# A planner's model of the chip: measured durations, tiling changes, DMA rate and clock, with due times fitted anew

## The chip, the cores and the metric

The kernel runs on one core of one Trainium2 chip. The core has TensorE (PE, matmuls; PEld is its weight load), VectorE (DVE), ScalarE (ACT), GpSimd (POOL) and SyncE (SP), which here issues every DMA. Each engine works through its own queue in order; a semaphore holds an instruction until its inputs are there, and everything behind it on that engine waits too. The metric is the device time of one execution in microseconds (us), lower is better; a profiled execution has a span, from its first to its last instruction.

## What is computed

A recurrent attention over 768 steps for 4 batches of 8 heads with head size 40, and then a two-branch MLP over the 3072 tokens:

```python
for t in range(S):                                   # S = 768, state (B, H, 40, 40)
    y[:, :, t] = einsum('bhd,bhde->bhe', rt, state)
    Sa = einsum('bhde,bhe->bhd', state, at)
    state = state * wt[:, :, None, :] - einsum('bhd,bhe->bhde', Sa, bt) + einsum('bhd,bhe->bhde', vt, kt)
x = y.transpose(0, 2, 1, 3).reshape(3072, 320)
out = ((x @ w1) * (x @ w2) @ w3) @ w_out             # 320 -> 1024 -> 1024 -> 320
```

The MLP weights arrive as 64-bit floats.

## The kernel before

The 768 steps are cut into 12 **chunks** of 64 steps; a chunk has 4 **groups** (one for each batch, 8 heads each). The work of the whole kernel is cut into a few thousand *ops*, each a handful of instructions on one engine:

- **Weight conversion** (`convert`, L277 to L301): 33 pieces of 128x512. SP loads `raw` (L277); DVE takes the exponent `e` (L280), the high mantissa (L290), adds the low word (L294) and forms the sign and exponent factor `sg` (L298); ACT does L284 and L287; POOL multiplies (L301). Four pieces are of w1 and w2, five of w_out, sixteen of w3, eight more of w1 and w2. PE multiplies w3 and w_out into one matrix (L354), and L341 makes the low halves of w1 and w2. No MLP can begin before all of this is done (the mark `W12`).
- **scale** (L384 to L411), for each group: running products of the decays `fm` on DVE, log and exponential on ACT (L393, L396), the scaled inputs `lh` and `fm` on DVE or POOL.
- **causal** (L436): products inside the chunk on PE; ACT copies them to `JP` and `lh`; POOL masks (L454).
- **solve** (L468 to L546), once a chunk: L468 transposes `JP` into `ab`, some fifty DVE instructions invert triangular blocks, L543 and L546 write `TDX`. **join** (L569, L576): PE and ACT make `TT` from it.
- **pairs** (L613) and **tokens** (L636): products and transposes that need no state.
- **rec**, for each group, the only part that carries the state from chunk to chunk: L652, L659, L666, L677 and the transpose L700 on PE, with ACT copies and the DVE steps L670, L694, L711 between.
- **mlp**, once a chunk: 16 sets of 8 matmuls 128x128 by 256 columns (L763), ACT and DVE steps on their results, 8 sets of 6 matmuls by 320 columns (L789), and the stores. Its input `xs` is made by ACT (L746) and DVE (L749) from what `gather` (L721) has brought together by DMA.

L176 is the copy helper of ACT. The PE array is used as a whole (L354, L636, L652, L700, L763, L789), as 128-row halves of 64 columns (L659, L677), as 64x64 quarters (L436, L613, L666) or as 32x32 blocks (L569, L576). Below, a **tiling change** is a place where two ops that follow each other on PE use the array in different ones of these four ways.

What sets the order is a **planner**, the class `Order`. All ops are first recorded with engine, cost, due time, what they read and write, and their buffers; `place` then plays the chip on the host: each engine has a clock, an op can start when its engine, its inputs and its buffers are free, and of the ops of an engine that could start first the one with the earliest due time is taken. An op marked `two` uses the SBUF port that DVE and POOL share and isn't planned beside one of the other engine. The sequence that comes out is fixed for each engine in the program. The core of it:

```python
first = min(t for t, _ in starts)
o = min((o for t, o in starts if t <= first + 1e-9), key=lambda o: (o["due"], o["n"]))
cost = o["cost"]
if e == "pe":
    cost += 0.1 * (o["kind"] != last)
clock[e] = t + cost
done = clock[e] + LAT[e]
u["ready"] = max(u["ready"], clock[e] if u["eng"] == e != "sp" else done)
```

Due times are a start per chunk (`T0 + T * c`) plus an offset per stage (the table `P`); a DMA is planned at 0.4 to 0.6 us with 3 us more until its data are there.

Of the kernel before, what the change touches and what calls it, by code (L numbers as in the profile page):

```python
# [18 lines left out]
C = 64  # L19
# [11 lines left out]
LAT = dict(pe=0.33, act=0.09, dve=0.09, pool=0.1, sp=3.0, nil=0.0)  # L31
# [9 lines left out]
ON = dict(cv="p", ws="d", lh="dpdddppdpdpp", xs="pppdpppdpppd", gl="pppdpppddddd")  # L41

# [14 lines left out]
class Order:  # L57
# [14 lines left out]
    def op(self, eng, cost, due, fn, r=(), w=(), two=False, kind=None, hold=()):  # L72
# [13 lines left out]
        for s in slots:  # L86
            s.left += 1
        self.ops.append(dict(n=n, eng=eng, cost=cost, due=due, fn=fn, deps=deps - {None, n}, slots=slots, two=two,
                             kind=kind))

    def place(self):
        ops = self.ops
        for o in ops:
            o["users"], o["wait"] = [], len(o["deps"])
        for o in ops:
            for d in o["deps"]:
                ops[d]["users"].append(o)
        free = {p: [(0.0, i) for i in range(n)] for p, n in SLOTS.items()}
        ready = {e: [] for e in LAT}
        clock, last, lock = dict.fromkeys(LAT, 0.0), None, {"dve": 0.0, "pool": 0.0}  # L100
        for o in ops:
            o["ready"] = 0.0
            if not o["wait"]:
                ready[o["eng"]].append(o)

        def begin(o):

            t, new = max(o["ready"], clock[o["eng"]]), {}
# [8 lines left out]
            if o["two"]:  # L117
                t = max(t, lock["pool" if o["eng"] == "dve" else "dve"])
            return t

        placed = []
        while len(placed) < len(ops):
            best = None
            for e in LAT:
                starts = [(t, o) for o in ready[e] if (t := begin(o)) is not None]
                if starts:
                    first = min(t for t, _ in starts)
                    o = min((o for t, o in starts if t <= first + 1e-9), key=lambda o: (o["due"], o["n"]))
                    if best is None or first < best[0]:
                        best = first, o  # L130
# [6 lines left out]
            if e == "pe":  # L137
                cost += 0.1 * (o["kind"] != last)
                last = o["kind"]
# [6 lines left out]
            if o["two"]:  # L146
                lock[e] = clock[e]
# [816 lines left out]
```

## Time and profile before

| | |
|---|---|
| time, median of 3 runs | 757.23 us (756.07 to 763.5) |
| span of the profiled execution | 757.2 us |
| PE busy / DVE / ACT / POOL | 84% / 79% / 62% / 32% |
| moved by DMA | 70.44 MB, 93 GB/s over the span |
| mean granted TensorE clock | 0.966 |

The profiled execution's own time and its span are the same number within 0.1 us, and both are the median of the runs. Busy shares are averages over a first part, in which weights are converted beside the first chunks, and a second, in which MLP and attention share PE. Times of an instruction in a timeline are from its start on its engine to its end; matmuls are pipelined, so from one set of matmuls to the next the start times count, not the durations.

### The profile page before, as it was taken

The page shows a single profiled execution, that of the slowest core. Times are in us where ns is not written, and L with a number is a line of the kernel's source. Part 1 is how long each engine was busy: PE and PEld are TensorE (multiplying, and loading weights), DVE is VectorE, ACT ScalarE, POOL GpSimd, SP SyncE. Part 2 cuts the span into 40 slices and gives each one's busy share as a digit, 9 for nine tenths or more (in the row PEclk, how much of TensorE's full clock was granted, in tenths as well). Part 3 has the DMA queues.
Part 4 walks back from the last instruction along what each step waited for, and adds up shares of the span by engine and source line. Part 5 has one row for each costly group of instructions (what it writes and reads, how often), then busy time and mean ns, then how long its engine had stood idle before and what let it go on. Part 6 is the DMA issues. An engine that isn't in the chain of part 4 may idle for free.

```text
span 757.2 us, 22430 instructions
## 1 busy us (share of the span) xinstructions
PE 635.4 (84%) x9106; PEld 565.1 (75%) x9106; DVE 598.8 (79%) x1177; ACT 471.3 (62%) x1127; POOL 245.1 (32%) x326
## 2 busy tenths in 40 slices
PE   0411198874889999999999999999999999999996
PEld 0301176653778898898898889888989889999996
DVE  5779979999989995995887979969788789595421
ACT  2653486655876577687676785867757767646321
POOL 2444454333324142353341323715324213100000
PEclk9999999876779999999999999999999999999999
DMA  8922257433340241433333323333343243120010
GB/s 212 262 68 94 84 140 226 138 102 112 102 122 16 55 124 51 116 84 81 96 91 101 83 73 104 85 83 84 82 107 91 66 103 100 40 57 23 11 35 21
DMA packets 57947, 70.44 MB, mean 93 GB/s; under 512 B 30960, under 2 KB 38640, under 8 KB 57840
## 3 DMA queue, kind: packets, MB, share of 16 engines
q1 hardware_dynamic: 57840, 68.97, 33.7%
q8 instruction: 73, 1.20, 0.7%
q14 instruction: 34, 0.28, 0.1%
HBM read 60.29 MB, written 3.93 MB: 85 GB/s over the span
## 4 chain that ended last, share of the span: by engine, by line
PE 42%; DVE 23%; ACT 4%; DMA 4%; issue 3%; SPq 1%; POOL 0%; DVEq 0%; POOLq 0%; ACTq 0%
PE bank L763 16%; PE bank L789 7%; DVE tmp L494 3%; DMA fm<-in_fmx_dram 3%; PE bank L659 3%; PE bank L652 3%; PE bank L677 3%; PE bank L666 3%; DVE xu L670 2%; PE bank L613 2%; PE bank L436 2%; PE bank L636 2%; PE bank L700 1%; ACT TT L176 1%; DVE ab L468 1%
## 5 line engine op out<-in xcount | busy, mean ns | idle before, releaser
L763 PE MATMUL bank<-xs,W 128*128 128x256 f32 x1536 | 212.1, 288 | 3.4 <-DVE ga L777 1.4
L763 PEld LDWEIGHTS bank<-xs,W 128*128 128x128 f32 x1536 | 189.2, 189 | 10.3 <-DVE ga L777 1.7
L176 ACT ACTIVATE xu<-bank 64x256 f32<-64x256 f32 (+2 forms) x184 | 80.0, 440 | 25.6 <-PE bank L613 13.0
L454 POOL TENSOR_SCALAR_AFFINE_SELECT lh<-lh 64x256 f32<-64x256 f32 x96 | 44.4, 462 | 149.5 <-ACT lh L176 125.0
L176 ACT ACTIVATE JP<-bank 32x256 f32<-32x256 f32 (+1 forms) x216 | 75.5, 350 | 14.3 <-PE bank L436 10.3
L670 DVE TENSOR_TENSOR xu<-bank,mask_h 64x416 f32<-64x416 f32 x96 | 56.2, 586 | 33.9 <-PE bank L666 31.8
L621 POOL TENSOR_SCALAR_AFFINE_SELECT xu<-xu 64x256 f32<-64x256 f32 x96 | 43.9, 457 | 111.1 <-ACT xu L176 91.0
L411 POOL TENSOR_TENSOR fm<-fm,gi 104x512 f32<-104x512 f32 x36 | 51.2, 1423 | 45.2 <-DVE gi L407 36.6
L659 PE MATMUL bank<-xu,lh 104*64 104x104 f32 (+2 forms) x768 | 50.6, 272 | 16.4 <-POOL xu L621 14.2
L789 PE MATMUL bank<-W3h,gh 128*128 128x320 f32 x192 | 64.2, 334 | 0.0
L436 PE MATMUL bank<-lh,fm 40*64 40x64 f32 x1536 | 38.5, 240 | 26.6 <-POOL fm L411 23.4
L789 PE MATMUL bank<-W3l,gh 128*128 128x320 f32 x192 | 59.3, 309 | 0.0
L789 PE MATMUL bank<-W3h,gl 128*128 128x320 f32 x192 | 59.1, 308 | 0.0
L613 PE MATMUL bank<-rv 40*64 40x64 f32 x768 | 34.5, 232 | 27.9 <-DMA rv<-in_rv_dram 18.7
L659 PEld LDWEIGHTS bank<-xu,lh 104*64 104x64 f32 (+2 forms) x768 | 40.4, 146 | 23.2 <-POOL xu L621 15.0
L436 PEld LDWEIGHTS bank<-lh,fm 40*64 40x64 f32 x1536 | 31.4, 148 | 33.1 <-POOL fm L411 24.0
L777 DVE TENSOR_TENSOR ga<-bank,ga 128x512 f32<-128x512 f32 x48 | 32.8, 684 | 27.4 <-PE bank L763 25.9
L613 PEld LDWEIGHTS bank<-rv 40*64 40x64 f32 x768 | 27.7, 141 | 35.7 <-DMA rv<-in_rv_dram 18.0
L284 ACT ACTIVATE e<-e,ebias 128x512 uint16<-128x512 uint16 x33 | 23.3, 717 | 47.2 <-DVE e L280 47.1
L666 PE MATMUL bank<-hs,TT 64*64 64x104 f32 x768 | 47.4, 268 | 4.7 <-ACT TT L176 2.1
L176 ACT ACTIVATE gh<-ga 128x512 fp32r<-128x512 f32 x48 | 30.1, 627 | 33.5 <-DVE ga L777 33.4
L176 ACT ACTIVATE ga<-bank 128x512 f32<-128x512 f32 x48 | 28.6, 595 | 31.6 <-PE bank L763 31.3
(96 smaller groups left out, 1448.6 us busy)
## 6 DMA issues: line engine op xcount, KB each, us to landing
fm<-in_fmx_dram SPq DMA_DIRECT2D x48, 313.6 KB
rv<-in_rv_dram SPq DMA_DIRECT2D x48, 273.0 KB
lh<-in_fma_dram SPq DMA_DIRECT2D x48, 208.0 KB
raw<-in_w3t_dram SPq DMA_DIRECT2D x16, 512.0 KB
raw<-in_w_dram SPq DMA_DIRECT2D x12, 512.0 KB
xu<-in_vt_dram SPq DMA_DIRECT2D x96, 40.0 KB
out_dram<-o SPq DMA_DIRECT2D x48, 80.0 KB
xr<-y SPq DMA_DIRECT2D x72, 40.0 KB
```

Source lines behind the costliest of these rows:

```text
L176: act.activation(out_, in_, AF.Copy, scale=scale)
L411: e.tensor_tensor(out=X, in0=X, in1=gi.t.unsqueeze(2).to_broadcast([104, NP, 2, C]), op=ALU.mult)
L436: pe.matmul(out=bank(ab)[64 * x:64 * x + 64, p], lhsT=X[r, p, x], rhs=lh.t[r, ab, p], start=True, stop=True)
L454: pool.affine_select(out=lh.t[q, ab], in_=lh.t[q, ab], pattern=[[0, NP], [1, C]], compare_op=ALU.is_gt, fill=0.0, base=0, channel_multipli ...
L613: pe.matmul(out=bank()[64 - 64 * ab:128 - 64 * ab, p, 0:C], lhsT=rvt.t[r, p, C + D:], rhs=rvt.t[r, p, 0:C], start=True, stop=True)
L621: op("pool", 0.5, due + 2, lambda q=q, ab=ab: pool.affine_select(out=xu.t[q, ab, :, 0:C], in_=xu.t[q, ab, :, 0:C], pattern=[[0, NP], [1, C ...
L659: pe.matmul(out=view(hp)[64 * ab:64 * ab + 64, p], lhsT=lh.t[k, ab, p], rhs=xu.t[k, ab, p], start=True, stop=True)
L666: pe.matmul(out=view(hh)[r, p], lhsT=tt.t[r, n0 + p], rhs=hs.t[r, p], start=True, stop=True)
L670: dve.tensor_tensor(out=xu.t[r, ab], in0=view(hh)[r], in1=mask_h[r].unsqueeze(1).to_broadcast([64, NP, N]), op=ALU.mult)
L763: pe.matmul(out=pt.t[:, TOK * x:TOK * x + TOK], lhsT=WT[k][:, cs], rhs=xs.t[:, z], start=(n == 0), stop=(n == 7))
L777: op("dve", 0.65, t, lambda a=a, pt=pt: dve.tensor_tensor(out=a.t, in0=wide(pt), in1=a.t, op=ALU.mult), r=[pt], w=[a])
L789: pe.matmul(out=pt.t[:, 0:DM], lhsT=l.t[:, j, ts], rhs=W3[r][:, j], start=(j == 0 and n == 0), stop=(j == NJ - 1 and n == 2))
```

## The change

No instruction of the computation is changed, nor how many there are of one, nor on which engine it is, nor a buffer count. Changed are the numbers and rules by which `place` orders them: a table `OPS` gives each of some seventy kinds of op its duration (and for PE the way it uses the array and the time to its last result); a table `OFF` adds an offset to the due time of each kind; `LAT` has a lag for each pair of engines; a DMA occupies its queue for a time that follows its bytes; a PE op in another tiling has to wait until the one before is finished (`turn`) and pays an entry (`ENTRY`); and the planned PE has two clock levels, set by how busy its plan has been. Of ops that could start within `LOOK` of the first (0.092 us on PE, 0.046 us on POOL), the one due first is taken. `T0`, `T` and `P` have new values. All calls of `op` name a kind in place of engine and cost.

```diff
-LAT = dict(pe=0.33, act=0.09, dve=0.09, pool=0.1, sp=3.0, nil=0.0)
-T0, T = 29.92, 49.86
-P = dict(w0=13.0, ws=3.12, ld=74.57, sc=51.76, ca=50.45, so=7.57, sp=36.91, jo=6.89, pa=12.28, tk=4.63, rg=14.44,
-         ga=35.51, ml=82.44, mt=47.69)
+T0, T = 37.797, 51.192
+P = dict(w0=11.454, ws=3.321, ld=32.264, sc=51.261, ca=85.143, so=7.546, sp=49.375, jo=113.483, pa=26.202, tk=12.035,
+         rg=12.467, ga=112.137, ml=87.719, mt=49.172)
+OFF = {"ca.jd": -119.786, "ca.jo": -52.948, "ca.lh": 12.039, "ca.mask": -5.365, "ca.mm": -117.544, "cv.e": 6.804,
+       "cv.exp": 61.542, "cv.f": 6.953, "cv.in": 36.478, "cv.lo": 13.503, "cv.m": -184.82, "cv.out/p": -153.603,
...
+LOOK = dict(pe=0.092, act=0.0, dve=0.0, pool=0.046, sp=0.0, nil=0.0)
...
+OPS = {
+    "cv.in": ("sp", 2.23), "cv.e": ("dve", 0.415, 1), "cv.exp": ("act", 0.72), "cv.sign": ("act", 0.66),
...
+    "ld.fm": ("sp", 1.4), "ld.lh": ("sp", 0.93),
...
+    "r.mm2": ("pe", 0.714, 0, "c64", 0.884), "r.hs": ("act", 0.517), "r.mm3": ("pe", 0.71, 0, "64", 0.88),
...
+ENTRY = {"128": 0.09, "c64": 0.04, "64": 0.04, "32": 0.0}
...
-            t, new = max(o["ready"], clock[o["eng"]]), {}
+            t, new = max(o["ready"], turn if e == "pe" and o["mode"] != last else clock[e]), {}
...
-                    o = min((o for t, o in starts if t <= first + 1e-9), key=lambda o: (o["due"], o["n"]))
+                    t, o = min(((t, o) for t, o in starts if t <= first + LOOK[e]), key=lambda x: (x[1]["due"], x[1]["n"]))
...
-            cost = o["cost"]
-            if e == "pe":
-                cost += 0.1 * (o["kind"] != last)
-                last = o["kind"]
+            if e == "pe":
...
+                f = 1 if hot else 2
+                begun = t + f * ENTRY[o["mode"]] * (o["mode"] != last)
+                done, last = begun + f * o["span"], o["mode"]
+                clock[e], turn = begun + f * o["cost"], done - 0.07
...
-        op("dve", 0.4, due, f1, w=[G])
-        op("dve", 0.72, due, f2, w=[G], two=True)
+        op("sc.min", due, f1, w=[G])
+        op("sc.scan", due, f2, w=[G])
```

The changed file is 55 lines longer from the table on: L384 of before is L439 of the changed one, and so on with every line below.

Where the order differs, in three places. **ACT, before its copies into `JP` for the third and fourth group of the first chunk** (L176 is the copy, L284 and L287 belong to the weight conversion, L393 and L396 to scale). Before:

```order
L284 ACTIVATE e_153<-e_153,ebias 128x512
L176 ACTIVATE xu_119<-bank_140 64x4x64
L393 ACTIVATE gi_110<-fm_100 104x256
L396 ACTIVATE gi_110,stats<-gi_110 104x256
L176 ACTIVATE JP_129<-bank_142 32x256
L176 ACTIVATE JP_129<-bank_142 32x4x32
L176 ACTIVATE JP_129<-bank_143 32x256
L176 ACTIVATE JP_129<-bank_143 32x4x32
L176 ACTIVATE lh_106<-bank_142 64x256
L176 ACTIVATE lh_106<-bank_143 64x256
```

Changed, at the fourth group (L235 is the copy, L342 the sign of the first piece of weights, L448 and L451 are scale):

```order
L448 ACTIVATE gi_111<-fm_101 104x256
L451 ACTIVATE gi_111,stats<-gi_111 104x256
L235 ACTIVATE JP_129<-bank_141 32x256
L235 ACTIVATE JP_129<-bank_142 32x256
L342 ACTIVATE sg_154<-raw_147 128x512
L235 ACTIVATE JP_129<-bank_141 32x4x32
L235 ACTIVATE JP_129<-bank_142 32x4x32
L235 ACTIVATE lh_107<-bank_141 64x256
L235 ACTIVATE lh_107<-bank_142 64x256
```

Before, the conversion's sixth L284 stands ahead of the copies; changed, no L284 does, and one sign (L342) stands between them.

**DVE, up to the transpose that begins the first solve** (L280 is the exponent of a piece of weights, L384, L389, L403 and L407 are scale, L468 the transpose). Before:

```order
L280 TENSOR_SCALAR e_152<-raw_147 128x512
L389 SCALAR_TENSOR_TENSOR fm_100<-fm_100,first 104x260
L280 TENSOR_SCALAR e_153<-raw_148 128x512
L389 SCALAR_TENSOR_TENSOR fm_101<-fm_101,first 104x260
L384 TENSOR_SCALAR fm_102,stats<-fm_102 104x260
L384 TENSOR_SCALAR fm_103,stats<-fm_103 104x260
L389 SCALAR_TENSOR_TENSOR fm_102<-fm_102,first 104x260
L389 SCALAR_TENSOR_TENSOR fm_103<-fm_103,first 104x260
L403 TENSOR_TENSOR gt_112<-fm_100,gi_110 104x256
L407 SCALAR_TENSOR_TENSOR gi_110<-gt_112,gi_110 104x256
L468 STREAM_TRANSPOSE ab<-JP_129 128x1024
```

Changed:

```order
L444 SCALAR_TENSOR_TENSOR fm_102<-fm_102,first 104x260
L455 TENSOR_TENSOR lh_105<-lh_105,fm_97 104x512
L455 TENSOR_TENSOR lh_106<-lh_106,fm_98 104x512
L462 SCALAR_TENSOR_TENSOR gi_111<-gt_112,gi_111 104x256
L455 TENSOR_TENSOR lh_107<-lh_107,fm_99 104x512
L458 TENSOR_TENSOR gt_112<-fm_100,gi_110 104x256
L444 SCALAR_TENSOR_TENSOR fm_103<-fm_103,first 104x260
L462 SCALAR_TENSOR_TENSOR gi_110<-gt_112,gi_110 104x256
L523 STREAM_TRANSPOSE ab<-JP_129 128x1024
```

Before, 17 instructions of the weight conversion (6 of L280, 4 of L290, 4 of L294, 3 of L298) stand ahead of the first solve; changed, none does, and the scale instructions ahead of it are the same in number.

**PE, early in the MLP of the fifth chunk, when the rec steps of the sixth begin** (L666, L659, L677, L700 are rec, L613 pairs, L636 tokens). Before:

```order
L666 MATMUL bank_141<-hs_124,TT_132 64x104 x8
L659 MATMUL bank_139<-xu_118,lh_108 64x104 x8
L677 MATMUL bank_138<-xu_119,bk_122 40x104 x8
L666 MATMUL bank_142<-hs_123,TT_132 64x104 x8
L700 MATMUL bank_139<-ident,st_125 40x104 x4
L677 MATMUL bank_143<-xu_117,bk_120 40x104 x8
L613 MATMUL bank_141<-rv_116 64x64 x8
L677 MATMUL bank_140<-xu_118,bk_121 40x104 x8
L700 MATMUL bank_138<-ident,st_126 40x104 x4
```

Changed (L714, L732, L721, L668, L755 and L691 are L659, L677, L666, L613, L700 and L636 of before):

```order
L714 MATMUL bank_142<-xu_118,lh_108 64x104 x8
L732 MATMUL bank_143<-xu_119,bk_122 40x104 x8
L732 MATMUL bank_139<-xu_117,bk_120 40x104 x8
L721 MATMUL bank_138<-hs_123,TT_132 64x104 x8
L668 MATMUL bank_140<-rv_116 64x64 x8
L755 MATMUL bank_142<-ident,st_125 40x104 x4
L755 MATMUL bank_143<-ident,st_126 40x104 x4
L691 MATMUL bank_139<-ident,fm_103 128x104 x4
L691 MATMUL bank_140<-ident,fm_96 128x104 x4
```

The nine rows of before hold seven tiling changes, the nine of the changed order two: ops that use the array in the same way have moved together.

## Rows read from the trace of the kernel before

**Rows 1.** The page: busy time of each engine, and in 40 slices of the span the busy tenths of DVE and the granted clock of PE in tenths.

```profile
PE 635.4 (84%) x9106; PEld 565.1 (75%) x9106; DVE 598.8 (79%) x1177; ACT 471.3 (62%) x1127; POOL 245.1 (32%) x326
...
DVE  5779979999989995995887979969788789595421
...
PEclk9999999876779999999999999999999999999999
```

**Rows 2.** Busy time of each engine in four stretches: to the first solve's transpose, to the first MLP matmul, to the last chunk's MLP, and that MLP. Columns: stretch, length, busy us (instructions) by engine, granted clock, share of the DMA engines, GB/s.

```profile
0.00:45.40 45.40, 9.84 (x188) 8.35 (x188) 28.46 (x59) 22.02 (x56) 15.50 (x28) 1.00 0.77 209
45.40:223.30 177.90, 111.02 (x1304) 85.72 (x1304) 166.51 (x306) 103.98 (x233) 74.93 (x85) 0.87 0.41 120
223.30:727.70 504.40, 491.80 (x7436) 448.80 (x7436) 396.86 (x802) 339.27 (x829) 154.63 (x214) 1.00 0.30 77
727.70:757.20 29.50, 22.76 (x178) 22.27 (x178) 6.98 (x12) 6.07 (x11) 0.00 (x0) 0.94 0.08 20
```

**Rows 3.** Timeline of DVE up to the first solve, rows with idle time before them (in brackets: how long, and what ended it). Columns: start, duration, engine, line, operation.

```profile
15.72 0.42 DVE L384 TENSOR_SCALAR_CACHE_REDUCE fm<-fm 104x260 f32<-104x260 f32 x1 [3.65 <-DMA fm<-in_fmx_dram]
...
19.61 0.42 DVE L384 TENSOR_SCALAR_CACHE_REDUCE fm<-fm 104x260 f32<-104x260 f32 x1 [3.46 <-DMA fm<-in_fmx_dram]
...
39.49 0.43 DVE L280 TENSOR_SCALAR e<-raw 128x512 uint16<-128x512 uint16 x1 [3.75 <-DMA raw<-in_wo_dram]
...
45.45 1.96 DVE L468 STREAM_TRANSPOSE ab<-JP 128x1024 f32<-128x1024 f32 x1 [2.21 <-ACT JP L176]
```

**Rows 4.** Timeline of ACT at the same place.

```profile
39.95 0.72 ACT L284 ACTIVATE e<-e,ebias 128x512 uint16<-128x512 uint16 x1 [3.67 <-DVE e L280]
...
41.81 1.30 ACT L176 ACTIVATE JP<-bank 32x256 f32<-32x256 f32 x4
```

**Rows 5.** Groups of DVE instructions before 45.4 us, those of the weight conversion (busy us, mean ns of one, then idle before them).

```profile
L294 DVE SCALAR_TENSOR_TENSOR mf<-raw,mf 128x512 f32<-128x512 uint32 x4 | 4.7, 1180 | 0.1
...
L280 DVE TENSOR_SCALAR e<-raw 128x512 uint16<-128x512 uint16 x6 | 2.5, 418 | 5.3 <-DMA raw<-in_wo_dram 5.3
...
L290 DVE TENSOR_SCALAR mf<-raw 128x512 int32<-128x512 int32 x4 | 1.7, 415 | 0.0
```

**Rows 6.** The page's DMA issues with their sizes.

```profile
fm<-in_fmx_dram SPq DMA_DIRECT2D x48, 313.6 KB
...
lh<-in_fma_dram SPq DMA_DIRECT2D x48, 208.0 KB
...
raw<-in_w_dram SPq DMA_DIRECT2D x12, 512.0 KB
```

**Rows 7.** Groups of DVE instructions from 0 to 223 us.

```profile
L294 DVE SCALAR_TENSOR_TENSOR mf<-raw,mf 128x512 f32<-128x512 uint32 x33 | 34.8, 1053 | 1.0
L290 DVE TENSOR_SCALAR mf<-raw 128x512 int32<-128x512 int32 x33 | 20.9, 635 | 0.0
...
L407 DVE SCALAR_TENSOR_TENSOR gi<-gt,gi 104x256 f32<-104x256 f32 x13 | 8.7, 672 | 0.9
...
L403 DVE TENSOR_TENSOR gt<-fm,gi 104x256 f32<-104x256 f32 x13 | 7.6, 582 | 0.0
```

**Rows 8.** Timeline of DVE in a stretch in which POOL did nothing, the same four lines once each.

```profile
91.97 0.38 DVE L403 TENSOR_TENSOR gt<-fm,gi 104x256 f32<-104x256 f32 x1
92.45 0.42 DVE L407 SCALAR_TENSOR_TENSOR gi<-gt,gi 104x256 f32<-104x256 f32 x1
...
93.13 0.42 DVE L290 TENSOR_SCALAR mf<-raw 128x512 int32<-128x512 int32 x1
93.58 0.69 DVE L294 SCALAR_TENSOR_TENSOR mf<-raw,mf 128x512 f32<-128x512 uint32 x1
```

**Rows 9.** Timeline of DVE and POOL together, one meeting of the two.

```profile
53.80 1.27 POOL L301 TENSOR_TENSOR mf<-mf,sg 128x512 f32<-128x512 f32 x1 [2.86 <-DVE sg L298]
54.09 1.52 DVE L294 SCALAR_TENSOR_TENSOR mf<-raw,mf 128x512 f32<-128x512 uint32 x1
```

**Rows 10.** Timeline of all engines at the start of the first MLP: the last low half of the weights, the MLP's input, its first matmuls.

```profile
218.24 0.69 DVE L341 TENSOR_TENSOR W<-mf,W 64x512 fp32r<-64x512 f32 x1 [0.23 <-ACT W L176]
...
220.19 0.84 ACT L746 ACTIVATE xs<-xr 128x768 fp32r<-128x768 f32 x1
...
223.35 0.86 PE L763 MATMUL bank<-xs,W 128*128 128x256 f32 x5 [0.34 <-ACT SB L176]
```

**Rows 11.** PE in one stretch of 4 us before that: busy us (instructions), granted clock (0.50 is 1.2 GHz, 1.00 is 2.4 GHz), share of the DMA engines, GB/s.

```profile
208.00:212.00 4.00, 3.55 (x21) 0.50 0.48 143
```

**Rows 12.** Timeline of PE in the stretch that MLP and attention share, and at the end.

```profile
299.01 1.64 PE L666 MATMUL bank<-hs,TT 64*64 64x104 f32 x32
300.59 0.58 PE L636 MATMUL bank<-ident,fm 104*128 104x104 f32 x4
...
310.54 0.93 PE L666 MATMUL bank<-hs,TT 64*64 64x104 f32 x16
311.40 1.21 PE L763 MATMUL bank<-xs,W 128*128 128x256 f32 x8
312.54 0.68 PE L613 MATMUL bank<-rv 40*64 40x64 f32 x16
...
728.70 15.22 PE L763 MATMUL bank<-xs,W 128*128 128x256 f32 x127 [0.61 <-DVE xs L749]
```

**Rows 13.** The page's group of the DVE step L670, two of which stand between L666 and L677 of each group.

```profile
L670 DVE TENSOR_TENSOR xu<-bank,mask_h 64x416 f32<-64x416 f32 x96 | 56.2, 586 | 33.9 <-PE bank L666 31.8
```

More of the change, by code (lines that the diff above doesn't have):

```diff
@@ L87, in op @@
             s.left += 1
-        self.ops.append(dict(n=n, eng=eng, cost=cost, due=due, fn=fn, deps=deps - {None, n}, slots=slots, two=two,
-                             kind=kind))
+        eng, took, *more = OPS[tag]
+        more += [0, None, 0.0][len(more):]
+        self.ops.append(dict(n=n, tag=tag, eng=eng, cost=took if cost is None else cost, due=due + OFF.get(tag, 0.0), fn=fn,
+                             deps=deps - {None, n}, slots=slots, two=more[0] if two is None else two, mode=more[1],
+                             span=more[2]))
     def place(self):
@@ L97, in place @@
                 ops[d]["users"].append(o)
+        engines = ("pe", "act", "dve", "pool", "sp", "nil")
         free = {p: [(0.0, i) for i in range(n)] for p, n in SLOTS.items()}
[L99 to L104, printed above, removed]
+        ready = {e: [o for o in ops if o["eng"] == e and not o["wait"]] for e in engines}
+        clock, turn, last, lock = dict.fromkeys(engines, 0.0), 0.0, None, {"dve": 0.0, "pool": 0.0}
         def begin(o):
-            t, new = max(o["ready"], clock[o["eng"]]), {}
+            e = o["eng"]
+            t, new = max(o["ready"], turn if e == "pe" and o["mode"] != last else clock[e]), {}
             for s in o["slots"]:
@@ L323, in weights @@
                     w3f = slot("w3f")
-                    for f in range(1024 // CW):
+                    for f in range(DFF // CW):
                         cs = slice(CW * f, CW * f + CW)
@@ L328, in weights @@
                     product(ib, w3f, due)
-                op("nil", 0.0, due, second, w=["reg2"])
-            for f in range(2048 // CW):
+                op("nil", due, second, w=["reg2"])
+            for f in range(2 * DFF // CW):
                 cs = slice(CW * f, CW * f + CW)
@@ L341, in f2 @@
                     e.tensor_tensor(out=WT[2 + k][rows, cs], in0=mf.t[rows], in1=WT[n][rows, cs], op=ALU.subtract)
[L343 to L344 removed]
+                op("w.hi", due, f1, r=[mf, *over], w=[("W", k, f)])
+                both(ON["ws"], "w.lo", due, f2, r=[mf, *over], w=[("W", k, f)])
                 due += step
[L346 removed]
+        op("nil", due, third, r=[("W", k, f) for k in range(3) for f in range(4)], w=["W12", "conv"])
     def product(ib, w3f, due):
@@ L720, in move @@
         def move(dst, src):
-            op("sp", 0.6, due, lambda: sp.dma_start(out=dst(), in_=src()), r=[(y, g) for g in range(B)], w=[(xr, n[0])])
+            op("ga", due, lambda: sp.dma_start(out=dst(), in_=src()), r=[(y, g) for g in range(B)], w=[(xr, n[0])])
             n[0] += 1
```

214 lines of the change are left out of this document (129 added, 85 removed).

## The prediction

> **What bounds the kernel now.** I read the page first, and in it the 40 slices. PE is the busiest engine over the span, but the slices show two stages: up to about slice 12 DVE stands at nine tenths nearly throughout, and there the granted clock of PE falls to six and seven tenths; behind it PE's clock is full to the end [rows 1]. So I asked for busy times in four stretches [rows 2]. From the first solve to the first MLP matmul (45.4 to 223.3 us) DVE is busy for 166.5 of 177.9 us and PE for 111.0. From there to the last chunk's MLP (504.4 us) PE is busy for 491.8 us, DVE for 396.9. The last 29.5 us are one MLP that nothing can stand beside. The reader is to see that the kernel is bound by DVE until the first MLP, by PE behind that, and that the first MLP's start is the seam: PE's work behind it is nearly the same in both orders, so whatever brings the seam forward is gained in full.
>
> The third view is the timeline of the start. Up to the first solve DVE is busy for only 28.5 of 45.4 us [rows 2]. It waits 3.65 and 3.46 us for `fm` and 3.75 us for a piece of w_out, and then 2.21 us for ACT's copies into `JP` [rows 3]. ACT was held by that same piece of w_out: its L284 at 39.95 us waited 3.67 us for DVE's L280, and the copies into `JP` began behind it at 41.81 us [rows 4]. Two queues in order carried a late DMA into a chain that has no use for it.
>
> **What the change does to the first solve.** The changed order has no conversion ahead of it on DVE. Of the 28.5 us of DVE's work, L294, L280 and L290 there are 4.7 + 2.5 + 1.7 = 8.9 us [rows 5], which leaves 19.6 us. SP now issues all eight `fm`, then six `lh` with three pairs of small `xu`, then the first piece of weights, whose sign stands between ACT's last copies. These are 8 x 313.6 + 6 x 208 + 512 = 4269 KB [rows 6], 4.5 MB with the `xu`; at the 209 GB/s of the first stretch [rows 2] that takes 21.6 us, and with the first issue and the last copies I put the solve at 24 us, an estimate. DVE's idle time is then 24 - 19.6 = 4.4 us in place of 45.4 - 28.5 = 16.9, a gain of 12.5 us; the conversion work isn't gone but runs beside the solve. I take **12 us**. The lower end is 5: the two waits for `fm` may stay in another form, and only 3.75 + 2.21 us go. The upper end is 15.
>
> **Waiting of DVE for POOL.** In the first 223 us an L294 takes 1053 ns on average, an L290 635, an L407 672, an L403 582 [rows 7]; where POOL is still, the same take 0.69, 0.42, 0.42 and 0.38 us [rows 8]. One meeting shows why: POOL's L301 began at 53.80 us, DVE's L294 at 54.09 us, and it took 1.52 us, ending half a microsecond behind POOL's 55.07 [rows 9]. The excess is 33 x 0.363 + 33 x 0.215 + 13 x 0.252 + 13 x 0.202 = 12.0 + 7.1 + 3.3 + 2.6 = 25 us. Both planners keep such ops apart, but the old one has its clock only roughly right, and an error anywhere lets them meet. With measured durations they should meet less. How much less no row shows: between nothing, or 5 us more, and 20 us less, I take 40% of the excess, **10 us**, since even an exact plan has to put POOL's 74.9 us beside DVE's 166.5 in 177.9 [rows 2]: 63.5 us have to overlap.
>
> On this the Trainium skill's page SBUF — State Buffer (section SBUF: two separate sides) says that the pair of ports that DVE and GpSimd share is an exclusive lock: who starts first holds it for the whole instruction, and the other blocks. By that rule 25 us of waiting could not shrink by more than POOL's work finds partners that need no shared pair, the solve above all; the meeting at 53.80 us agrees with it. It speaks for a share, not for the whole.
>
> **To the seam.** The conversions, scale steps and solves ahead of the first MLP input on DVE are the same in number in both orders, up to seven small solve instructions, one L411 and one L694 that now follow; I count these at nothing. From the last low half of the weights (218.24 + 0.69 = 218.9 us) over the input on ACT (220.19) to the first matmul (223.35) [rows 10] there are 4.4 us that I leave as they are. The first MLP then begins at 223.35 - 12 - 10 = 201 us.
>
> **PE behind the seam.** Counted in the whole order of PE, there are 366 tiling changes before and 271 now; behind the first L763 308 and 226, so 82 fewer. What one costs is read from start to start [rows 12]. Alone among ops of other tilings, a set of 8 L763 takes 312.54 - 311.40 = 1.14 us, where the last MLP has 15.22 / 127 x 8 = 0.96: 0.18 us for going in and out. On the other side a single group of L666 takes 311.40 - 310.54 = 0.86 us, two in a row 300.59 - 299.01 = 1.58, so 0.14 us saved by standing together. A way there and back, two changes, costs 0.32 us: 0.16 each, and 82 x 0.16 = **13 us**. PE has 504.4 - 491.8 = 12.6 us of idle time in this stretch; I leave it as it is, with 8 us less and 15 more as the bounds, because ops that stand together also ask for their copies together. The last MLP keeps its 29.5 us: its input now has five MLP sets and eight of L789 of the chunk before as cover, where it had four and eight.
>
> **The sum**, against the profiled span of 757.2 us, which is also the median of the runs: 757.2 - 12 - 10 - 13 = **722 us**. With each term at its ends and not all at once (5 to 15, -5 to 20, 8 to 15, and idle time from +15 to -8), the forecast's own range is 706 to 738.
>
> **Rivals.**
>
> *The seam doesn't move with DVE* (739 us). PE has 111 us of work between the first solve and the seam, much of it at 1.2 GHz: at 208 us the granted clock is 0.50 with PE busy for 3.55 of 4 us [rows 11]. If DVE is done earlier, the rec steps of the second chunk, which stand ahead of the first L763 in PE's queue, become the end of the stage, each at the slow clock and each behind ACT. For it: the last 4.4 us before the seam already run over ACT and PE. Against: PE is idle for 67 of the 178 us. I give the first stage 5 of its 22 us then: 757.2 - 5 - 13 = 739.
>
> The Trainium skill's page TensorE: Matmul & The Clock Gate (section The HAM clock gate, What's actually happening) says that the slow clock is the default and activity releases it. A shorter stage with the same PE work would by that rule be warmer, and this rival less likely; no row of before shows PE in a shorter first stage.
>
> *Bunched rec steps starve PE* (769 us, slower). Where L666, L659 and L677 stand together, the two L670 between L666 and L677 of a group (2 x 0.586 = 1.17 us [rows 13]) have less PE work in front of them. If PE had to wait them out for each of the 40 groups behind the seam, that is 47 us, and 722 + 47 = 769. It decides from 35 us on, 0.9 us for each group. Against it: in PE's order several other ops still stand between the two, and the idle time now is 0.3 us for each group.
>
> *The new plan holds no better than the old* (757 us). DMA landings or ACT drift from the plan as before, waits change places, and what the tiling changes give is lost in the start. For it: every engine runs in order, so one wrong duration stops all behind it. Against it: the 17 us of waiting ahead of the first solve go by order alone, whatever the plan's clock.
>
> **How the numbers follow.** Forecast 722: 0.68. Seam stays: 0.17. No better: 0.07. Starved: 0.05. The rest, 0.03, is below 706 (all ends at once would be near 700). The range from 704 to 746 holds the forecast and the seam rival and leaves out 0.15. About 1% is what a measurement of this kernel can tell from no change: 749.7 to 764.8 us. Faster by more is 0.87, within 0.08, slower 0.05.
>
> **What the changed profile would show.** The first solve's transpose (L523) at 22 to 27 us with no conversion ahead of it. An L349 (L294 of before) at 0.85 to 0.95 us on average in the first stage. The first L818 at 195 to 210 us. Behind that a stretch of about 491 us with PE idle for 8 to 25 us. I am wrong if the first L818 is behind 215 us, which would be the first rival, or if PE waits for L670 in long rows, which would be the second; and on the size of the tiling term if sets of L818 between other tilings don't take 1.14 us.

## The result, and the profile after

The changed kernel takes 718.15 us (median of four runs, 716.19 to 719.82) against 760.37 us (756.07 to 763.67) of the kernel before on the same chip: a ratio of 0.945, with a 95% interval from 0.940 to 0.950. The forecast was 722 us, 35 us below the profiled span of before; the two spans differ by 39.2 us, the two medians by 42.2.

The page of the profiled execution (span 718.0 us), the lines that answer to [rows 1]:

```profile
PE 616.6 (86%) x9106; PEld 557.7 (78%) x9106; DVE 570.3 (79%) x1177; ACT 470.3 (66%) x1127; POOL 251.6 (35%) x326
...
DVE  9699999986899886968969969689699698793331
...
PEclk9985689965999999999999999999999999999999
```

The instructions of PE and DVE are the same in number as in [rows 1], but PE is busy for 18.8 us less and DVE for 28.5 us less: the same work got shorter by the place it stands in. The same four stretches as in [rows 2], to the first solve, to the first MLP matmul, to the last chunk's MLP, and that MLP:

```profile
0.00:27.50 27.50, 7.05 (x140) 5.60 (x140) 19.79 (x42) 16.07 (x45) 13.34 (x29) 1.00 0.83 239
27.50:197.90 170.40, 107.62 (x1348) 84.52 (x1348) 155.61 (x313) 109.53 (x241) 83.34 (x82) 0.78 0.46 141
197.90:688.00 490.10, 478.70 (x7437) 444.90 (x7438) 387.93 (x811) 338.36 (x833) 154.87 (x216) 1.00 0.30 80
688.00:718.00 30.00, 23.24 (x184) 22.72 (x182) 7.00 (x12) 6.38 (x13) 0.00 (x0) 0.96 0.09 23
```

The seam, the first MLP matmul, moved from 223.35 to 197.96 us:

```profile
197.96 1.21 PE L818 MATMUL bank<-xs,W 128*128 128x256 f32 x8 [0.40 <-ACT bk L235]
```

That is 25.4 us. Behind it the stage is 520.0 us long in place of 533.9, 13.8 us less. In the first stage, up to the seam, DVE's time divides as follows (busy and idle from the two tables; the length of a stretch less its busy time is idle):

| us | before | after | difference |
|---|---|---|---|
| DVE idle up to the first solve | 16.9 | 7.7 | -9.2 |
| DVE idle from there to the seam | 11.4 | 14.8 | +3.4 |
| DVE busy up to the seam | 195.0 | 175.4 | -19.6 |

The groups of DVE from 0 to 198 us, to be held against [rows 7] (L349 is L294 of before, L345 is L290, L462 is L407, L458 is L403; L353 and L335 are L298 and L280):

```profile
L349 DVE SCALAR_TENSOR_TENSOR mf<-raw,mf 128x512 f32<-128x512 uint32 x33 | 29.0, 891 | 0.0
L353 DVE TENSOR_TENSOR sg<-sg,e 128x512 bf16<-128x512 bf16 x33 | 18.2, 569 | 2.9 <-ACT e L339 2.7
L335 DVE TENSOR_SCALAR e<-raw 128x512 uint16<-128x512 uint16 x33 | 17.1, 540 | 0.0
L345 DVE TENSOR_SCALAR mf<-raw 128x512 int32<-128x512 int32 x33 | 13.6, 444 | 0.0
...
L458 DVE TENSOR_TENSOR gt<-fm,gi 104x256 f32<-104x256 f32 x13 | 7.4, 567 | 2.2 <-ACT gi L451 2.2
...
L462 DVE SCALAR_TENSOR_TENSOR gi<-gt,gi 104x256 f32<-104x256 f32 x13 | 5.5, 427 | 0.0
```

The four groups that the prediction priced lost 5.8 + 7.3 + 3.2 + 0.2 = 16.5 us. L353 and L335 gained 2.8 and 1.5 us (L298 and L280 took 15.4 and 15.6 us before): they now meet POOL where L345 did before. The six groups together lost 12.2 us. And some of the waiting has changed sides. POOL's weight products L356 take 51.4 us in the first stage where L301 took 41.1; POOL's busy time as a whole grew from 90.4 to 96.7 us there. The longest of them, on POOL, with DVE's rows beside it:

```profile
60.26 6.03 POOL L356 TENSOR_TENSOR wof<-mf,sg 128x512 f32<-128x512 f32 x1 [4.65 <-DVE sg L353]
...
60.03 1.09 DVE L335 TENSOR_SCALAR e<-raw 128x512 uint16<-128x512 uint16 x3
...
64.85 0.42 DVE L462 SCALAR_TENSOR_TENSOR gi<-gt,gi 104x256 f32<-104x256 f32 x1
65.19 0.69 DVE L549 TENSOR_TENSOR tmp<-ab,DG 128x512 f32<-128x512 f32 x1
```

Thirteen DVE instructions stand without a gap from 60.03 to 65.27 us, all of conversion and scale; the product, some 1.2 us of work, ends at 66.29, about one product's length behind the last of them. DVE lost nothing here, and the solve step L549 that follows, one of whose inputs (`ab`) lies in PSUM, ran beside POOL at its usual 0.69 us. In [rows 9] it was DVE that waited.

### The profile page after: what moved, and what is told of

Its sections match the earlier page's. It is cut to its first block, busy times and chain, and to the rows that moved or that the text cites. A ratio compares the mean times of both kernels' runs of the same rounds, so it can differ in the third digit from the quotient of the medians.

```text
span 718.0 us, 22449 instructions
## 1 busy us (share of the span) xinstructions
PE 616.6 (86%) x9106; PEld 557.7 (78%) x9106; DVE 570.3 (79%) x1177; ACT 470.3 (66%) x1127; POOL 251.6 (35%) x326
## 4 chain that ended last, share of the span: by engine, by line
PE 54%; DVE 16%; ACT 16%; issue 5%; DMA 3%; POOL 3%; SPq 2%; ACTq 0%; DVEq 0%; POOLq 0%
PE bank L818 23%; PE bank L844 5%; ACT JP L235 5%; PE bank L714 4%; ACT TT L235 4%; PE bank L721 4%; PE bank L732 4%; PE bank L707 3%; PE bank L491 3%; DVE mf L349 3%; PE bank L409 2%; PE bank L755 2%; PE bank L691 2%; ACT lh L235 2%; SPq L776 2%
## 5 line engine op out<-in xcount | busy, mean ns | idle before, releaser
L818 PE MATMUL bank<-xs,W 128*128 128x256 f32 x1536 | 209.9, 288 | 1.2 <-ACT bk L235 0.4
L235 ACT ACTIVATE xu<-bank 64x256 f32<-64x256 f32 (+2 forms) x184 | 81.2, 442 | 52.8 <-PE bank L668 25.6
L235 ACT ACTIVATE JP<-bank 32x256 f32<-32x256 f32 (+2 forms) x216 | 75.6, 350 | 18.3 <-PE bank L491 15.5
L509 POOL TENSOR_SCALAR_AFFINE_SELECT lh<-lh 64x256 f32<-64x256 f32 x96 | 42.8, 446 | 94.8 <-ACT lh L235 83.5
L491 PE MATMUL bank<-lh,fm 40*64 40x64 f32 x1536 | 40.1, 242 | 37.4 <-POOL fm L466 30.5
L725 DVE TENSOR_TENSOR xu<-bank,mask_h 64x416 f32<-64x416 f32 x96 | 56.3, 586 | 14.5 <-PE bank L721 13.1
L714 PE MATMUL bank<-xu,lh 104*64 104x104 f32 (+2 forms) x768 | 47.6, 266 | 13.4 <-POOL xu L676 10.0
L235 ACT ACTIVATE gh<-ga 128x512 fp32r<-128x512 f32 x48 | 30.1, 627 | 39.0 <-DVE ga L832 38.7
L714 PEld LDWEIGHTS bank<-xu,lh 104*64 104x64 f32 (+2 forms) x768 | 37.9, 141 | 19.8 <-POOL xu L676 11.0
L409 PE MATMUL bank<-wof,w3f 128*128 128x320 f32 x128 | 44.1, 502 | 6.2 <-POOL w3f L356 5.5
L721 PE MATMUL bank<-hs,TT 64*64 64x104 f32 x768 | 45.8, 263 | 3.9 <-ACT TT L235 1.8
L835 POOL TENSOR_TENSOR gl<-ga,gh 128x512 fp32r<-128x512 f32 x24 | 32.5, 1354 | 45.6 <-ACT gh L235 43.8
L523 DVE STREAM_TRANSPOSE ab<-JP 128x1024 f32<-128x1024 f32 x12 | 23.8, 1987 | 30.7 <-ACT JP L235 30.7
L721 PEld LDWEIGHTS bank<-hs,TT 64*64 64x64 f32 x768 | 37.5, 139 | 10.1 <-ACT TT L235 2.6
```

The lines of the kernel that those rows point to most:

```text
L235: act.activation(out_, in_, AF.Copy, scale=scale)
L409: pe.matmul(out=pt.t[:, 0:DM], lhsT=w[:, j], rhs=wof[:, j], start=(j == 0), stop=(j == NJ - 1))
L491: pe.matmul(out=bank(ab)[64 * x:64 * x + 64, p], lhsT=X[r, p, x], rhs=lh.t[r, ab, p], start=True, stop=True)
L509: pool.affine_select(out=lh.t[q, ab], in_=lh.t[q, ab], pattern=[[0, NP], [1, C]], compare_op=ALU.is_gt, fill=0.0, base=0, channel_multipli ...
L714: pe.matmul(out=view(hp)[64 * ab:64 * ab + 64, p], lhsT=lh.t[k, ab, p], rhs=xu.t[k, ab, p], start=True, stop=True)
L721: pe.matmul(out=view(hh)[r, p], lhsT=tt.t[r, n0 + p], rhs=hs.t[r, p], start=True, stop=True)
```

## The experiments

**The order joined from two halves.** Here the planner's result is written out as a list `PLAN`, and the kernels differ in that list alone. Their lines stand 31 further down than those of the changed kernel: L266 is the copy of ACT in them, L554 the first solve's transpose. The control has the changed order; the other three take a first part from one order and what is left, in its own sequence, from the other.

```diff
-        while len(placed) < len(ops):
+        ops, plan = self.ops, list(PLAN)
+        while plan:
...
+PLAN = struct.unpack("<3710H", ...)
```

> The changed order, op by op, written down as a list in place of the planner, so that orders can be joined; only which of several equal buffers an op gets is decided anew. Every theory expects 718 us within 1%; the next three are read against it.

> The order of before up to the first MLP matmul, the changed order behind it. Theory (two stages whose gains add): first L818 at about 223 us, 520 us behind it, 743 us in all. Rival (the gain behind the seam needs the new start, since buffers and DMAs are left in another state): more than 750 us.

> The changed order up to the first MLP matmul, the order of before behind it. Theory: first L818 at about 198 us, 534 us behind it, 732 us in all, with PE busy for some 13 us more behind the seam than in the changed kernel. Rival (the new start only moves waiting behind the seam): 745 us or more.

> The order of before up to the transpose of the first solve, the changed order behind it. Theory (DVE's idle time ahead of the first solve is gained in full, 16.9 us before and 7.7 in the changed kernel): first solve at 45 us, the first L818 9 us later than in the changed kernel, 727 us in all. Rival (later waits of the first stage take the gain up again): first L818 within 3 us of the changed kernel's, 718 to 721 us.

| order | time (us) | ratio to before, 95% | first solve | seam | behind the seam |
|---|---|---|---|---|---|
| control | 718.2 | 0.946 (0.939 to 0.953) | 27.5 | 193.8 | 522.3 |
| old up to the seam | 742.4 | 0.975 (0.967 to 0.983) | 46.4 | 226.1 | 519.1 |
| old behind the seam | 735.3 | 0.969 (0.960 to 0.976) | 27.5 | 193.5 | 535.4 |
| old up to the first solve | 732.0 | 0.963 (0.955 to 0.971) | 46.1 | 207.4 | 521.9 |

The stage behind the seam in the control (columns as in [rows 2]):

```profile
193.80:716.10 522.30, 503.39 (x7618) 468.66 (x7618) 392.32 (x823) 345.24 (x843) 154.77 (x216) 0.99 0.29 76
```

With the old order there:

```profile
193.54:728.90 535.36, 515.30 (x7617) 472.24 (x7614) 407.64 (x821) 345.83 (x842) 155.71 (x216) 0.99 0.28 74
```

Behind the same seam the old order keeps PE busy for 11.9 us more and takes 13.1 us longer. So the two stages' gains are separate and add: 24.2 us (742.4 - 718.2) and 17.1 us (735.3 - 718.2), 41.3 in all, beside the 40.2 us between control and before in that comparison (758.4). Inside the first stage 13.8 us hang on the order ahead of the first solve (732.0 - 718.2) and 10.3 us on what stands between there and the seam (742.4 - 732.0). These shares are rough: the runs of the three joined orders scatter by 6 to 9 us, those of the old order up to the seam from 737.5 to 746.9, and by the seams of the profiled executions the two shares of the first stage are 13.6 and 18.7 us.

The old order up to the first solve cost more than the 9 us that were expected. Against the control DVE is idle for 9.2 us more up to the first solve, for 2.1 us more from there to the seam, and busy for 2.3 us more; only the first of these was in the sum.

**The model alone, the due times alone.** The first has the new `OPS`, `LAT`, `ENTRY`, `LOOK` and the clock, with the old due times; the second the old planner with the new ones.

```diff
-T0, T = 37.797, 51.192
+T0, T = 29.92, 49.86
-OFF = {"ca.jd": -119.786, "ca.jo": -52.948, ...
+OFF = {}
```
```diff
-        self.ops.append(dict(n=n, eng=eng, cost=cost, due=due, fn=fn, deps=deps - {None, n}, slots=slots, two=two,
+        self.ops.append(dict(n=n, eng=eng, cost=cost, due=due + SHIFT[KIND[n]], fn=fn, deps=deps - {None, n}, slots=slots, two=two,
```

> The planner's new model (durations, lags, tiling changes, DMA rate, clock, LOOK) with the old due times (T0, T, P of before, no OFF). Its order has 113 ops ahead of the first solve where the changed kernel has 111 and the old one 152, and 279 tiling changes behind the first MLP matmul where they have 226 and 308. If the model brings the gain: first solve at 24 to 29 us, seam near 200, behind the seam 29 x 0.16 = 5 us less than before, so about 757 - 22 - 5 = 730 us. If the gain is in the due times that were fitted anew: 750 us or more, with the first solve still early (the order puts it there) but the seam behind 215 us.

> The old planner's costs and lags with the new due times (T0, T, P and OFF). Its order has all 33 conversions ahead of the first solve. If due times only mean something together with the model that they were fitted to: about 800 us, with the first solve behind 100 us and the second stage waiting for the state of the chunks. If the due times carry the gain by themselves: below 745 us.

The model alone takes 730.2 us (0.960 of before, 0.957 to 0.964), with the first solve at 27.6 us and the seam at 190.9. That seam has fewer attention ops ahead of it, 1332 PE instructions in place of the control's 1488, so the stage behind it is longer, 540.9 us where some 528 had been expected, and the two halves can't be set beside the control's one by one: the total came as expected, its parts didn't. The due times alone take 819.5 us (1.077, 1.072 to 1.083), with the first solve at 140.0 us; behind the seam, at 202.4 us, PE is idle for 58.9 of 614.7 us. The model carries some 30 us of the 42, and the offsets are worth something only together with the model that they were fitted to. Which part of the model carries it (the durations, the lags, the DMA's time, the tiling rule, the clock or `LOOK`) was not tested.

**The price of a tiling change by itself.** A probe behind all work of the changed kernel, on PE alone, with operands that have long been there:

```diff
+        for _ in range(40):
+            whole()
+            quarter()
+        for _ in range(20):
+            whole()
+            whole()
+            quarter()
+            quarter()
+        for _ in range(40):
+            whole()
+        for _ in range(40):
+            quarter()
```

> The changed kernel, and behind all of its work a probe on PE alone: 40 times a set of eight 128x128 matmuls by 256 columns and a set of sixteen 64x64 matmuls by 64 columns in turn (80 tiling changes), then the same work in pairs, 20 times two sets and two sets (40 changes), then 40 sets of the one and 40 of the other (1 change). If a change costs 0.16 us, the first block is 6.4 us longer than the second and 12.8 us longer than the last two together. If it costs nothing by itself, and what the trace of before showed was waiting for inputs, all three take the same time.

Timeline of PE: where the three blocks begin, and what follows the last (L930 are whole sets, L936 quarters):

```profile
711.34 1.07 PE L930 MATMUL bank<-xs,W 128*128 128x256 f32 x8
...
799.99 2.15 PE L930 MATMUL bank<-xs,W 128*128 128x256 f32 x16
...
881.86 4.39 PE L930 MATMUL bank<-xs,W 128*128 128x256 f32 x35
...
957.22 0.19 PE L974 MATMUL bank<-good,ones 128*1 128x1 f32 x2
```

From start to start the blocks take 88.65, 81.87 and 75.36 us. The first has 40 changes more than the second and 79 more than the third: 6.78 / 40 = 0.170 and 13.29 / 79 = 0.168 us each, at the full clock (granted 1.00 in all three). This is one execution of the probe.

**POOL's weight product left out, in both orders.** POOL writes a constant where it multiplied; everything else is in its old place.

```diff
-            e.tensor_tensor(out=mf.t[:, 0:n] if dst is None else dst(), in0=mf.t[:, 0:n], in1=sg.t[:, 0:n], op=ALU.mult)
+            e.memset(mf.t[:, 0:n] if dst is None else dst(), 0.01)
```

> The changed kernel, in which POOL's product of each piece of weights is left out: POOL writes a constant into the same place instead, so the MLP runs with constant weights. The order of all ops stays. If the long DVE instructions of the first stage are meetings with POOL's reads: L349 falls from 891 ns to 0.70 to 0.75 us on average (33 x 0.17 = 5 us less), L345 from 444 ns to 0.42, the seam comes 4 to 8 us earlier and the time is 710 to 714 us. If they are long for another reason (the stride of raw, the transfers), L349 stays at 0.85 us or more and the time at 716 to 718.

> The kernel before with the same product left out and a constant in its place; the order of all ops stays. If meetings with POOL cost the old order more than the new one, it gains more here: L294 from 1053 ns to 0.8 us or less and L290 from 635 ns to 0.5 us or less, 8 + 4 = 12 us in the first stage, and some of the meetings with scale steps stay; 743 to 748 us. If both orders gain the same (5 us, 752 to 755 us), the meetings with this product are not what the change removed.

The changed order takes 698.9 us (0.923 of before, 0.918 to 0.929), 19 us less, where 4 to 8 had been expected; the old one 743.2 us (0.979, 0.975 to 0.984), 17 us less. The expectation for the changed order had priced L349 and L345 alone. The seams are at 178.3 and 206.1 us. Changed order, DVE's groups and the first stage:

```profile
L349 DVE SCALAR_TENSOR_TENSOR mf<-raw,mf 128x512 f32<-128x512 uint32 x33 | 22.1, 684 | 0.0
L335 DVE TENSOR_SCALAR e<-raw 128x512 uint16<-128x512 uint16 x33 | 13.6, 432 | 0.0
L353 DVE TENSOR_TENSOR sg<-sg,e 128x512 bf16<-128x512 bf16 x33 | 13.5, 420 | 3.8 <-ACT e L339 2.3 <-ACT sg L342 1.4
...
0.00:178.34 178.34, 105.83 (x1489) 84.15 (x1489) 157.65 (x355) 125.43 (x285) 65.45 (x110) 0.95 0.56 172
```

Old order:

```profile
L294 DVE SCALAR_TENSOR_TENSOR mf<-raw,mf 128x512 f32<-128x512 uint32 x33 | 27.7, 840 | 1.0
...
L290 DVE TENSOR_SCALAR mf<-raw 128x512 int32<-128x512 int32 x33 | 13.8, 419 | 0.0
...
0.00:206.05 206.05, 111.85 (x1493) 87.75 (x1493) 174.99 (x363) 125.94 (x288) 67.08 (x112) 0.94 0.52 150
```

In the changed order every L349 now takes its unhindered 0.68 us, so its excess was meetings with the product and nothing else. But the expected difference between the orders isn't there: without the product DVE is busy for 17.8 us less in the changed order (175.46 to 157.65) and for 20.0 us less in the old one (195.02 to 174.99). Meetings with this product cost both about the same, and 17.3 us of DVE's time still separate the two without it. Some 4 of these are ten instructions (eight of the solve, a scan and a scale product) that the new order has behind the seam. Much of the rest are meetings with POOL's other work, scale products and masks: L294 stays at 840 ns in the old order, because five of its 33 took 1.63 us, each of them beside a scale product L411. Taking the product out also moves all that follows in time, so the two shares can't be parted to the microsecond.

An estimate from the traces of all five kernels agrees. For each DVE instruction up to the seam it takes the time over that of the quickest tenth of its kind, where that is 0.06 us or more, and looks which of POOL's instructions ran beside it; one of POOL's did in every case. In the last two columns a constant stands in the product's place. The third row is the time in which the records of successive DVE instructions overlap (three L335 of 0.42 us each stand in 1.09 us above):

| us, an estimate | before | changed | control | left out, old order | left out, changed order |
|---|---|---|---|---|---|
| beside the weight product | 21.3 | 18.6 | 18.6 | 3.9 | 1.5 |
| beside POOL's other work alone | 13.0 | 4.8 | 4.2 | 10.8 | 3.4 |
| overlap of successive records | 15.8 | 20.2 | 20.4 | 15.8 | 20.2 |

By it the change took 11 us of meetings off DVE, 8 of them with POOL's other work. With the 4 us of instructions that moved and 4 us more of overlap these are the 19.6 us.

**An earlier start.** Three kernels on the control's list. The first solve waited for POOL's product of the fourth group, which stood behind masks:

```profile
20.37 0.79 POOL L509 TENSOR_SCALAR_AFFINE_SELECT lh<-lh 64x256 f32<-64x256 f32 x1 [3.98 <-ACT lh L235]
...
22.42 1.25 POOL L466 TENSOR_TENSOR fm<-fm,gi 104x512 f32<-104x512 f32 x1
...
23.73 1.13 PE L491 MATMUL bank<-lh,fm 40*64 40x64 f32 x32 [3.22 <-POOL fm L466]
...
27.58 1.98 DVE L523 STREAM_TRANSPOSE ab<-JP 128x1024 f32<-128x1024 f32 x1 [6.15 <-ACT JP L235]
```

The edit on POOL; on ACT the copies into JP of the fourth group go ahead of three copies into `lh`, a scale step and a sign:

```diff
-L540 AFFINE_SELECT lh_104<-lh_104 64x256 x2
-L497 TENSOR_TENSOR fm_99<-fm_99,gi_111 104x512
+L497 TENSOR_TENSOR fm_99<-fm_99,gi_111 104x512
+L540 AFFINE_SELECT lh_104<-lh_104 64x256 x2
```

> The changed kernel's order with its start edited: POOL's product for the fourth group goes ahead of the masks of the first groups, and ACT's copies into JP of the fourth group ahead of three of the copies into lh, of a sign and of a scale step. By the times of the changed kernel the product can start at 21.4 us instead of 22.4, PE is done at 23.9, the copies at 25.3: first solve at 25.3 instead of 27.6. If idle time of DVE in the first stage is worth its length, seam and end come 2.3 us earlier: 716 us. If PE or ACT set the first stage by now, the time stays at 718.

It takes 719.2 us (0.947, 0.944 to 0.950): nothing gained. The solve is early, and the rows of DVE and POOL behind it show what took the gain:

```profile
24.93 1.94 DVE L554 STREAM_TRANSPOSE ab<-JP 128x1024 f32<-128x1024 f32 x1 [2.25 <-ACT JP L266]
...
27.59 4.04 DVE L376 TENSOR_SCALAR mf<-raw 128x512 int32<-128x512 int32 x3
...
27.93 1.18 POOL L486 TENSOR_TENSOR lh<-lh,fm 104x512 f32<-104x512 f32 x1
...
30.19 1.17 POOL L486 TENSOR_TENSOR lh<-lh,fm 104x512 f32<-104x512 f32 x1
...
34.31 1.27 POOL L387 TENSOR_TENSOR mf<-mf,sg 128x512 f32<-128x512 f32 x1 [2.95 <-DVE sg L384]
```

And the control at the same place:

```profile
27.54 1.99 DVE L554 STREAM_TRANSPOSE ab<-JP 128x1024 f32<-128x1024 f32 x1 [6.09 <-ACT JP L266]
...
30.25 1.09 DVE L376 TENSOR_SCALAR mf<-raw 128x512 int32<-128x512 int32 x3
...
33.58 1.27 POOL L387 TENSOR_TENSOR mf<-mf,sg 128x512 f32<-128x512 f32 x1 [3.50 <-DVE sg L384]
```

Three L376 (L345 of the changed kernel) met POOL's products of the second chunk and took 4.04 us in place of 1.09; the first weight product (L387) came 0.7 us later than in the control although the solve was 2.6 us earlier. The next kernel takes that meeting away, by sending POOL's products ahead of the masks:

```diff
-L540 AFFINE_SELECT lh_105<-lh_105 64x256 x2
-L540 AFFINE_SELECT lh_106<-lh_106 64x256 x2
 L497 TENSOR_TENSOR fm_100<-fm_100,gi_110 104x512
 L486 TENSOR_TENSOR lh_108<-lh_108,fm_100 104x512
-L540 AFFINE_SELECT lh_107<-lh_107 64x256 x2
 L486 TENSOR_TENSOR lh_109<-lh_109,fm_101 104x512
+L540 AFFINE_SELECT lh_105<-lh_105 64x256 x2
...
```

> The edited start of the run before last, in which three DVE steps behind the early solve took 4.04 us beside three POOL products of the second chunk (1.09 us in the control). Here these three POOL products go ahead of six masks, so that they run under the solve's transpose. If that one meeting ate the gain: the three steps take 1.1 to 2.1 us, DVE's busy time up to the seam is 175 to 177 us, the next weight product begins 1.5 to 2.5 us before the control's, and the time is 715 to 717 us. If the place where the stage is set is another one by now: DVE is earlier, but the time stays at 718 to 719.

717.3 us (0.944, 0.940 to 0.948), not to be told from the control. The three L376 took 1.70 us as expected, DVE was busy for 177.1 us up to the seam, but the first weight product began at 33.62 us: now DVE waited for ACT.

```profile
33.04 0.42 DVE L384 TENSOR_TENSOR sg<-sg,e 128x512 bf16<-128x512 bf16 x1 [1.92 <-ACT e L370]
```

ACT began that step at 32.30 us, as in the control, behind copies of the second chunk. The last kernel puts it ahead of them, and on DVE the three exponent steps that feed it ahead of three mantissa steps:

```diff
+L370 ACTIVATE e_151<-e_151,ebias 128x512
+L370 ACTIVATE e_152<-e_152,ebias 128x512
+L370 ACTIVATE e_153<-e_153,ebias 128x512
 L266 ACTIVATE JP_130<-bank_143 32x256
...
```

> The run before (early solve, POOL's products under its transpose), and ACT's exponential steps (L370) of the first three pieces of weights go ahead of its five copies of the second chunk and a sign; DVE's three exponent steps (L366) that feed them go ahead of three mantissa steps. In the run before DVE waited 1.92 us for the first L370, which began at 32.30 us, as in the control (32.33). If ACT's queue in order is what holds the start by now: L370 at about 29.7 us, the first weight product at about 31.7 in place of 33.6, and 1 to 2 us less at the seam and in the time, 715 to 716.5 us. If the gain is lost again behind it (later meetings, PE's slow clock), the product is early but the time stays at 717 to 719.

The product is early at last, and the time stays: 717.9 us (0.944, 0.941 to 0.946). Rows of this kernel at the first product, at the third solve, and at the low half of the weights that stands ahead of the last one:

```profile
31.59 1.20 POOL L387 TENSOR_TENSOR mf<-mf,sg 128x512 f32<-128x512 f32 x1 [1.70 <-DVE sg L384]
...
180.31 1.97 DVE L554 STREAM_TRANSPOSE ab<-JP 128x1024 f32<-128x1024 f32 x1
...
186.17 0.94 DVE L427 TENSOR_TENSOR W<-mf,W 64x512 fp32r<-64x512 f32 x1 [1.07 <-ACT W L266]
```

The same two in the control:

```profile
181.48 1.99 DVE L554 STREAM_TRANSPOSE ab<-JP 128x1024 f32<-128x1024 f32 x1
...
186.38 0.92 DVE L427 TENSOR_TENSOR W<-mf,W 64x512 fp32r<-64x512 f32 x1 [1.14 <-ACT W L266]
```

Of 2.0 us at the first product 1.2 are left at the third solve, and 0.2 at a step that waits for ACT in both; the seam is at 193.96 against 193.80. What took the lead is to be seen in DVE's busy time up to the seam (third pair of columns behind the length), in the control, and in the first, second and last of the three edits:

```profile
0.00:193.80 193.80, 108.92 (x1488) 85.54 (x1489) 174.82 (x355) 125.72 (x285) 96.81 (x110) 0.93 0.53 158
...
0.00:195.22 195.22, 109.28 (x1489) 85.75 (x1489) 179.59 (x355) 125.87 (x285) 97.04 (x110) 0.93 0.52 157
...
0.00:197.09 197.09, 113.81 (x1489) 89.25 (x1489) 177.06 (x355) 125.67 (x285) 97.84 (x110) 0.82 0.52 156
...
0.00:193.96 193.96, 111.00 (x1488) 87.48 (x1488) 177.42 (x355) 125.69 (x285) 97.29 (x110) 0.92 0.53 158
```

The same 355 instructions of DVE take 4.8, 2.2 and 2.6 us more than in the control; in the last kernel DVE is idle for 2.4 us less and busy for 2.6 us more. By the estimate above the meetings with POOL's other work grew by 5.0, 2.3 and 2.6 us, and those with the weight product not at all.

## Why the prediction was right, and where it wasn't

**The seam** was put at 201 us and came at 198, and at 193.8 in the control, which has the same order. Its reason, that what DVE saves ahead of it is gained in full, is borne out by the joined orders to within 3 us: wherever the seam is, from 193.8 to 226.1 us, the stage behind takes 519 to 522 us with the new order there, and 535 with the old.

**The first solve.** Forecast at 24 us, it came at 27.58, outside the 22 to 27 us that were named. The queue step failed in a place that was not looked at: the sum went by bytes to be loaded and by DVE, while POOL, in order, had masks ahead of the fourth group's product; with the product and ACT's copies moved ahead the solve came at 24.93. DVE's idle time fell by 9.2 us up to the solve and not by 12.5. That the worth of the earlier start came near 12 us nonetheless (13.8 by the joined orders) is luck, since 4.4 of these are later idle and busy time of DVE that the term did not contain.

**Waiting for POOL.** 10 us were forecast, 40% of the excess of four groups. These four gave 16.5 us, and two groups that were not priced gave 4.3 back; over all of DVE's instructions the meetings fell by 11 us, by the estimate above. So the size was right, and in part by luck, since the share of 40% had no row behind it. That DVE and POOL meet less is borne out. But the meetings that the prediction showed, with the weight product, hardly changed (the product costs DVE 18 us with the new order and 20 with the old); 8 of the 11 us are meetings with scale products and masks. And the prediction let DVE bear the waiting on its own, where in the new order POOL bears 10 us more in its weight products. An L349 takes 0.891 us, within the 0.85 to 0.95 that were named.

**To the seam** nothing was counted, and this is where the first stage differs most from the sum: some 4 us of DVE's instructions now follow the seam, and its instructions overlap by some 4 us more. DVE's idle time there grew by 3.4 us in the profiled execution; in the control it is 10.7 us, 0.7 less than before, so this isn't the order's. That the 22 us of the first stage came to 25.4 is thus a sum of misses that partly cancel: 2.8 us too much at the first solve, 9.6 too little in DVE's busy time, 3.4 of idle time not foreseen.

**Tiling.** 82 changes fewer at 0.16 us gave 13 us. PE's busy time fell from 491.8 to 478.7 in that stretch, 13.1 us, and the probe's 0.168 us would give 13.8; a set of eight between other tilings takes 1.14 us in the probe from start to start (713.41 to 714.55 us), as read from [rows 12], and 1.15 us in the changed kernel (424.74 to 425.89). Idle time, left at 12.6, is 11.4, and the last MLP has 30.0 us in place of 29.5.

**The rivals.** A seam that doesn't move with DVE is refuted in the large: leaving out POOL's product took 18 us off DVE (and 31 off POOL, which is idle for half of the stage) and moved the seam by 20 us, or by 15 against the control. In the small PE's clock has a share in it: with the same order and DVE's busy time within 0.7 us, the seam stood at 197.96 us at a granted clock of 0.81 and at 193.80 at 0.93. The shorter stage was thus at a lower clock than the 0.89 of before in the one execution and at a higher one in the other. The early starts of 1 to 2 us don't speak for this rival, since DVE's busy time grew by as much. Rec steps that starve PE: of the twelve largest sums of PE's waits behind the seam, 1.6 us the first of them, one names L725, which is L670 of before, with 0.5 us. A plan no better than the old is refuted by 718 us in the changed kernel and in the control.

## What to carry to other kernels

Where two engines hinder each other, an order decides which of their instructions meet and who waits. Here it took away the meetings with POOL's scale products and masks and left those with the weight products, and the groups that had met before gave part of the waiting to others: price all of them, on both engines, and not only those that are long in the old trace. When an early finish is moved by hand in a planned order, everything behind it meets at other times, and the gain of one step may go to the next meeting or the next queue in order: follow it to the stage's end before it is counted. A cost that is paid at each change of a mode can be read from starts in a mixed stretch and holds well when it is multiplied by a count from the order.

## What the runs showed of the hardware

One order gave two courses of PE's granted clock: in the first stage the changed kernel's profiled execution had 0.81 on average, with the seam at 197.96 us, and the control's, the same order, 0.93 with the seam at 193.80. At the end 2 of the 4 us were left (718.0 and 716.1). The four runs of the changed kernel itself show it too: 719.8 and 719.5 us at a mean granted clock of 0.944 and 0.946, 716.9 and 716.2 at 0.975 and 0.977. Differences of a few microseconds at the seam between single profiled executions are no evidence of a change.

A POOL instruction of 1.2 us can stand for 6 when DVE's conversion and scale steps follow each other without a gap: none of thirteen left it in. So the engine that waits isn't always served after the first instruction that it meets; in [rows 9], where it was DVE that waited, one meeting cost it 0.8 us.

A change between whole 128x128 matmuls and 64x64 quarters cost 0.17 us each with PE alone at work (80 changes against 40 and 1 with the same work: 88.65, 81.87 and 75.36 us).
